# mLSTM cell and GELU MLP: the second chunk's weights all split, their sums moved beside the scores, the squares filled by ScalarE

## The chip, the cores and the metric

The kernel runs on one core of a Trainium2 chip. The metric is the device time in microseconds of the whole program: before the change, 455.98 us as the median of three runs (455.89 to 456.37). The trace is of one profiled execution, which took 455.72 us; all positions in this text are microseconds from the start of its span.

The engines are named as the profile names them: PE (matrix multiply; PEld is its weight load), DVE (VectorE), ACT (ScalarE), POOL (GpSimd) and SP (SyncE, which issues most transfers).

## The reference

Two blocks follow each other, all in float32.

```python
# q, k, v, o_gate: (B=4, H=8, S=768, D=40); i_gate, f_gate: (4, 8, 768)
for t in range(S):                                   # mLSTM cell, state C, n, m for each (b, h)
    m_new = max(f_gate[t] + m, i_gate[t])
    f, i = exp(f_gate[t] + m - m_new), exp(i_gate[t] - m_new);  m = m_new
    C = f * C + i * outer(v[t], k[t]);  n = f * n + i * k[t]
    y[t] = sigmoid(o_gate[t]) * (C @ q[t]) / max(abs(n @ q[t]), 1)
x = y.transpose(0, 2, 1, 3).reshape(3072, 320)       # heads side by side: H * D = 320
h = x @ w_in                                         # (320, 2048)
out = (h * sigmoid(1.702 * h)) @ w_out               # (2048, 320)
```

## The kernel before

The sequence is cut into six chunks of 128 steps (`w` = 0 to 5). The recurrence is turned into products within a chunk and a state carried between chunks, so a chunk of all four batches gives 512 rows of x, and the MLP of chunk `w` is run while the cell of chunk `w + 1` is computed beside it.

Each chunk has two stages on PE. `up` computes h transposed, in eight units `j`, each of two blocks of 128 columns of w_in, 512 rows wide. `down` multiplies the hidden values by w_out, in blocks; between the blocks the hand-written table `attention(w + 1)` puts the next chunk's cell: the carry, the scores, the values, the seams that turn the cell's output into the operand `xT`, and `split_x` and `split_on`, which prepare it for the next `up`. In chunk 0 both stages use plain float32 passes (`up`, 16 blocks of `down`); from chunk 1 on they are `up_fast` and `down_fast`, the latter with seven products of half matrices in place of eight, for which `w_out` is replaced by sums of its quarters (`t1`, `t2`, `t4` and a changed `w01`, made by `weight_sums(n)` on GpSimd) and the hidden values by sums (`hidden_difference`, `hidden_sums`, `last_sums`).

`up_fast` splits both operands. A float32 matrix is written as a high part, a low part and a difference, each in a form that PE multiplies in one pass of 512 columns. The 320 rows of w_in are two full blocks of 128 (`k` = 0, 1) and a rest of 64; the columns come in four pieces `n` of 512, two units to a piece. For each column block there are four main passes (high times high and low times low, for both k) and four side passes (two for the rest, two for difference times difference), so a unit has 16 passes. Main and side have PSUM banks of their own. Even units take theirs from the pool `ps_a`, odd ones from `ps_m`, two and four tiles in all, so unit j takes the banks that unit j - 2 had. ACT copies the scaled side product to the tile `g`, DVE adds the main product to it in one `scalar_tensor_tensor`, and ACT applies the GELU in place (`gelu_fast`). In chunk 1 pieces 2 and 3 are not split yet (`LATE`); their units j = 4 to 7 have `whole_passes`, float32 passes of 256 columns on w_in and xT, and only the rest's side passes.

The splits of w_in: `split_high(n)` on ACT, `split_diff(n)` on DVE, `split_low(n, engine)`. Highs stay in SBUF, and so do lows, but for piece 2. There is no room for the differences and low 2 in all stages: `keep` writes them to DRAM rows (`w_row`, 512 KB each, issued from ACT's queue), `fetch_diff` and `fetch_low` read them back through SP's queue in each `down` for the next chunk, into rooms that `rooms(w)` takes from the pools `gp` (eight tiles) and `sp` (four). The pools' other users are the `g` tiles, xT and the sums. `keep_last` copies low 3 to a place of its own.

The queries and keys of the next chunk are loaded in a layout with rows for four-step groups (`load_squares`: `q_sq`, `k_sq`), completed by `fill_squares` (two copies of 32 partitions each) and turned by `block_transposes` into `kT` and `qT`, on DVE, between the units j = 2 to 6.

Everything is in the order in which the text issues it (`tc.manual_schedule`): each engine runs its own queue in order, and the program adds semaphore waits. Transfers from SP's and ACT's queues take eight completion semaphores in turn; a transfer's issue waits until the transfer that last had its semaphore has landed. `wait_for(x)` makes GpSimd wait until x is written, by a tiny copy into the tile `mark`.

Order in chunk 1 before: `split_diff(1)`, `split_low(1, V)`, then the units; after j = 0 `gates(2)` on DVE and a wait of GpSimd for its end; after j = 0 to 3 one `weight_sums(j)` each; after j = 1 the row writes of differences 0 and 1; the transposes after j = 2 to 6. In its `down`, `split_high(2)`. In chunk 2 the other splits of pieces 2 and 3 come before j = 0 and after j = 1, with their row writes, and `keep_last` after j = 2.

Of the kernel before, what the change touches and what calls it, by code (L numbers as in the profile page):

```python
# [8 lines left out]
FP = mybir.dt.float32  # L9
FR = mybir.dt.float32r  # L10
# [21 lines left out]
def kernel(  # L32
# [81 lines left out]
    def fill_squares(t):  # L114

        x = t[:, 32:].rearrange("r (m d) -> r m d", d=D)
        for i in (0, 64):
            V.tensor_copy(out=x[i + 32:i + 64, :, 0:D - 32], in_=x[i:i + 32, :, 32:D])
# [281 lines left out]
    def block_transposes(w, n):  # L400
        b, (to, name, src) = n // 2, ((kT, "kT", k_sq), (qT, "qT", q_sq))[n % 2]
        if b == 0:
            fill_squares(src)
# [272 lines left out]
    LATE = (2, 3)  # L676

    def rooms(w):

        if w == 1:  # L680
            for n in (0, 1):
                w_diff[w, n] = sp.tile([128, 2, 512], FR, tag="g", name="w_diff")
        for c in range(2):
            xT[w, c] = (sp if w == 1 else gp).tile([128, 3, 2, L], FP, tag="g", name="xT")
        if w == 1:
            return
        for n in LATE[0:2 if w == 2 else 1]:
            w_low[w, n] = gp.tile([128, 2, 512], FR, tag="g", name="w_low")
        for n in (0, 2, 1, 3):
            w_diff[w, n] = sp.tile([128, 2, 512], FR, tag="g", name="w_diff")  # L690
# [5 lines left out]
    def split_diff(n):  # L696
        V.scalar_tensor_tensor(out=w_diff[2 if n in LATE else 1, n], in0=w_high[n], scalar=-1.0 - 1.0 / BASE,
                               in1=w_in[n], op0=OP.mult, op1=OP.add)

    def split_low(n, engine):  # L700
        if n not in LATE:
            w_low[n] = win.tile([128, 2, 512], FR, tag="wa" if n else "wb", name="w_low")
        engine.tensor_tensor(out=w_low[2, n] if n in LATE else w_low[n], in0=w_in[n], in1=w_high[n], op=OP.subtract)
# [5 lines left out]
    def keep_late(n):  # L709
        keep(w_diff_row, n, w_diff[2, n])  # L710
        if n == 2:
            keep(w_low_row, n, w_low[2, n])

    def keep_last():
        w_low[3] = work.tile([128, 2, 512], FR, tag="wx", bufs=1, name="w_low")
        A.copy(out=w_low[3], in_=w_low[2, 3])
# [46 lines left out]
    def gelu_fast(w, j, i):  # L763
        g = gs[w, j][:, i, :]
        A.activation(out=g, in_=g, func=AF.Gelu_apprx_sigmoid)  # L765
# [4 lines left out]
    def up_fast(w, j):  # L770
# [4 lines left out]
        whole = w == 1 and n in LATE  # L775
# [9 lines left out]
        def passes(which, i):  # L785
            for m in which:
                dst, k, a, x = parts[m]
                T.matmul(dst[i], a(i), x, start=(k == 0), stop=(k == (1 if whole else 3)))  # L788

        def whole_passes(i):  # L790
            for k in range(2):
                for c in range(2):
                    T.matmul(main[i][:, c * W // 2:(c + 1) * W // 2], w_in[n][:, k, col(i)],  # L793
                             xT[w, c][:, k].rearrange("p b t -> p (b t)"), start=(k == 0 and c == 0),
# [314 lines left out]
```

## Time and profile before

| | |
|---|---|
| median of three runs | 455.98 us |
| the profiled execution | 455.72 us, span 454.0 us |
| busy | PE 446.6 us (98%), DVE 342.6 (75%), ACT 214.0 (47%), POOL 132.5 (29%) |
| `up` of chunk 1 | 109.17 to 142.71 |
| `up` of chunks 2, 3, 4, 5 | 32.16, 29.54, 29.38, 29.40 us long |
| one g sum on DVE (L816) | 684 ns |
| one side copy on ACT (L812), one GELU (L765) | 591 ns, 629 ns |
| a difference or low of a piece on DVE (L697, L703) | 1.21 to 1.22 us |

A stage of `up` runs from PE's first pass for that chunk to its last; the `down` stage follows at once. The windows of the trace give each engine's busy time in such a stage; a PE busy time short of the window is idle PE. An engine other than PE may be idle without cost. In the chain of waits each piece is what the next one waited for, followed back from the end. Durations of neighbours on one engine overlap a little, so pairs are given start to start where it matters: two g sums take 1.20 us, two transposes 1.90.

### The profile page before, as it was taken

The page shows a single profiled execution, that of the slowest core. Times are in us where ns is not written, and L with a number is a line of the kernel's source. Part 1 is how long each engine was busy: PE and PEld are TensorE (multiplying, and loading weights), DVE is VectorE, ACT ScalarE, POOL GpSimd, SP SyncE. Part 2 cuts the span into 40 slices and gives each one's busy share as a digit, 9 for nine tenths or more (in the row PEclk, how much of TensorE's full clock was granted, in tenths as well). Part 3 has the DMA queues.
Part 4 walks back from the last instruction along what each step waited for, and adds up shares of the span by engine and source line. Part 5 has one row for each costly group of instructions (what it writes and reads, how often), then busy time and mean ns, then how long its engine had stood idle before and what let it go on. Part 6 is the DMA issues. An engine that isn't in the chain of part 4 may idle for free.

```text
span 454.0 us, 12115 instructions
## 1 busy us (share of the span) xinstructions
PE 446.6 (98%) x4967; PEld 388.8 (86%) x4967; DVE 342.6 (75%) x681; ACT 214.0 (47%) x471; POOL 132.5 (29%) x126
## 2 busy tenths in 40 slices
PE   8999999999999999998999999999999999999997
PEld 6877887776889999877999888999888999888996
DVE  6788999989799786879786789686789666733522
ACT  5686779601746701465900465900465910366100
POOL 5101317000496602334620044610035520035000
PEclk9999999999999999999999999999999999999999
DMA  8999999038669027858606987405998505700000
GB/s 169 200 304 192 229 222 195 1 73 205 93 144 166 4 61 206 226 95 155 81 19 142 309 132 158 64 17 139 304 127 148 86 17 142 228 37 1 1 30 29
DMA packets 129224, 58.49 MB, mean 129 GB/s; under 512 B 102048, under 2 KB 122480, under 8 KB 129168
## 3 DMA queue, kind: packets, MB, share of 16 engines
q1 hardware_dynamic: 120080, 53.28, 53.9%
q10 hardware_dynamic: 8768, 4.28, 4.1%
q8 instruction: 39, 0.64, 0.7%
q0 software_dynamic: 320, 0.15, 0.2%
q14 instruction: 17, 0.14, 0.1%
HBM read 47.53 MB, written 10.16 MB: 127 GB/s over the span
## 4 chain that ended last, share of the span: by engine, by line
PE 89%; DMA 4%; DVE 4%; SPq 1%; issue 1%; ACT 0%; ACTq 0%; DVEq 0%
PE p_out L879 34%; PE p_h L788 26%; PE p_h L638 6%; PE p_out L825 4%; PE p_h L793 3%; PE p_c L614 3%; PE p_s L471 2%; PE p_o L515 2%; PE p_i L523 2%; PE p_h L647 2%; DMA w_row<-w_diff 2%; PE p_t L396 1%; PE p_s L460 1%; DMA k_sq<-in_k_dram 1%; DMA wt<-m_row 1%
## 5 line engine op out<-in xcount | busy, mean ns | idle before, releaser
L816 DVE SCALAR_TENSOR_TENSOR g<-p_h,g 128x512 f32<-128x512 f32 x80 | 52.4, 684 | 32.0 <-ACT g L812 17.1
L879 PE MATMUL p_out<-w_out_sb,g 128*128 128x160 f32 x480 | 69.0, 300 | 1.1 <-ACT g L812 1.1
L765 ACT ACTIVATE g<-g 128x512 f32<-128x512 f32 x80 | 50.2, 629 | 38.8 <-DVE g L816 38.7
L879 PEld LDWEIGHTS p_out<-w_out_sb,g 128*128 128x128 f32 x480 | 66.3, 190 | 2.0 <-ACT g L812 1.6
L847 POOL TENSOR_TENSOR g<-g 128x512 f32<-128x512 f32 x20 | 25.9, 1302 | 125.4 <-ACT g L765 125.4
L812 ACT ACTIVATE g<-p_h 128x512 f32<-128x512 f32 x80 | 46.8, 591 | 30.6 <-PE p_h L788 28.5
L747 ACT ACTIVATE x_high<-xT 128x512 fp32r<-128x512 f32 x10 | 6.3, 631 | 112.6 <-DVE xT L584 112.6
L884 DVE TENSOR_TENSOR o_sb<-o_sb,p_out 128x160 f32<-128x160 f32 x70 | 21.1, 317 | 42.3 <-PE p_out L879 42.2
L788 PE MATMUL p_h<-x_rest,w_rest 128*128 128x512 f32 x160 | 50.4, 400 | 0.8 <-ACT g L812 0.7
L879 PE MATMUL p_out<-t_sb,s 128*128 128x160 f32 x320 | 47.1, 300 | 0.0
L879 PEld LDWEIGHTS p_out<-t_sb,s 128*128 128x128 f32 x320 | 44.4, 190 | 0.2
L788 PE MATMUL p_h<-x_low,w_low 128*128 128x512 f32 x144 | 43.9, 390 | 0.6 <-DVE x_low L757 0.6
L788 PE MATMUL p_h<-x_high,w_high 128*128 128x512 f32 x144 | 44.3, 394 | 0.0
L788 PE MATMUL p_h<-x_diff,w_diff 128*128 128x512 f32 x144 | 44.3, 394 | 0.0
L447 ACT ACTIVATE wt<-wt,cols 128x64 f32<-128x64 f32 x160 | 38.8, 333 | 0.1
L788 PEld LDWEIGHTS p_h<-x_rest,w_rest 128*128 128x128 f32 x160 | 29.7, 188 | 8.6 <-ACT g L812 1.1
L825 PE MATMUL p_out<-w_out_sb,g 128*128 128x320 f32 x128 | 35.7, 436 | 0.0
L788 PEld LDWEIGHTS p_h<-x_low,w_low 128*128 128x128 f32 x144 | 26.9, 188 | 6.7 <-DVE x_low L757 1.0
L788 PEld LDWEIGHTS p_h<-x_diff,w_diff 128*128 128x128 f32 x144 | 27.1, 188 | 6.3
L825 PEld LDWEIGHTS p_out<-w_out_sb,g 128*128 128x128 f32 x128 | 23.9, 190 | 9.6
L788 PEld LDWEIGHTS p_h<-x_high,w_high 128*128 128x128 f32 x144 | 26.8, 188 | 6.0 <-ACT x_high L747 0.4
L638 PE MATMUL p_h<-xT,w_in 128*128 128x256 f32 x128 | 29.6, 384 | 0.0
(194 smaller groups left out, 801.3 us busy)
## 6 DMA issues: line engine op xcount, KB each, us to landing
w_diff<-w_row SPq DMA_DIRECT2D x14, 512.0 KB, 4.5
wt<-m_row SPq DMA_DIRECT2D x20, 256.0 KB, 5.6
bits<-in_moe_w_in_dram SPq DMA_DIRECT2D x8, 512.0 KB, 8.7
out_dram<-o_sb SPq DMA_DIRECT2D x24, 160.0 KB, 2.4
q_sq<-in_q_dram SPq DMA_DIRECT2D x10, 320.0 KB, 7.8
eo<-in_o_gate_dram SPq DMA_DIRECT2D x5, 640.0 KB, 7.1
bits<-in_moe_w_out_dram SPq DMA_DIRECT2D x8, 320.0 KB, 5.9
q_sq<-x_row SPq DMA_DIRECT2D x10, 256.0 KB, 3.2
```

What stands on the lines that cost most here:

```text
L447: A.activation(out=x[:, h, :], in_=x[:, h, :], func=AF.Exp, scale=-1.0, bias=cols[w][:, c * PH + h:c * PH + h + 1])
L614: T.matmul(pc[i * 64:i * 64 + 64, x, j * D1:(j + 1) * D1], k_cols(w, t, c * PH + 2 * j + i), vw[w, c][t, 2 * j + i, :], start=True, stop=True)
L638: T.matmul(ph[j][i][:, t], w_in[f // 4][:, c, f % 4 * 128:f % 4 * 128 + 128], x[:, c, t], start=(first and c == 0 and n == 0), stop=(not f ...
L765: A.activation(out=g, in_=g, func=AF.Gelu_apprx_sigmoid)
L788: T.matmul(dst[i], a(i), x, start=(k == 0), stop=(k == (1 if whole else 3)))
L793: T.matmul(main[i][:, c * W // 2:(c + 1) * W // 2], w_in[n][:, k, col(i)], xT[w, c][:, k].rearrange("p b t -> p (b t)"), start=(k == 0 and ...
L812: A.activation(out=g[:, i, :], in_=side[i], func=AF.Copy, scale=-BASE)
L816: V.scalar_tensor_tensor(out=g[:, i, :], in0=main[i], scalar=1.0 if whole else 1.0 + 1.0 / BASE, in1=g[:, i, :], op0=OP.mult, op1=OP.add)
L825: T.matmul(po, gs[w, f // 2][:, f % 2, b * L:(b + 1) * L], w_out_sb[:, f, :], start=(f == 0), stop=(f == NF - 1))
L847: G.tensor_tensor(out=a10, in0=a00, in1=a10, op=OP.subtract)
L879: T.matmul(po, a(f), b[:, f, :], start=(f == 0), stop=(f == NH - 1))
L884: V.tensor_tensor(out=dst, in0=x, in1=po, op=OP.add)
```

## The change

Chunk 1 has no whole passes any more: pieces 2 and 3 are split in it, after j = 0 and j = 2 (highs) and after j = 1 and j = 2 (differences and lows, both on DVE), into four further `gp` tiles (`more_rooms`), which the g tiles of j = 4 to 7 take over afterwards. All five row writes are issued in chunk 1, after j = 1 (d0, d1), j = 2 (d2, l2) and j = 3 (d3), and `keep_last` after j = 3. Chunk 2 fetches everything back, as later chunks do.

`weight_sums` 0 and 1 go to chunk 0's `down` after block 8, sum 3 to after its block 12, each behind a `wait_for`; sum 2 follows j = 3 of chunk 1, behind a wait for low 3. `fill_squares` is done by ACT, for the keys after j = 1 and for the queries after j = 3 (in chunk 0, before block 0 of `down`). The output copies of chunk 0's `down` are done by ACT. In `up_fast` both side copies of a unit are issued before the GELUs of the unit before, where one GELU stood between them. Unit 0 takes its passes in the order 0, 1, 4, 6, 2, 7, 3, 5 (main 0 to 3 are high, high, low, low; side 4 to 7 are rest, rest, difference, difference) in place of 0, 1, 4, 2, 3, 5, 6, 7.

```diff
@@
 
         x = t[:, 32:].rearrange("r (m d) -> r m d", d=D)
         for i in (0, 64):
-            V.tensor_copy(out=x[i + 32:i + 64, :, 0:D - 32], in_=x[i:i + 32, :, 32:D])
+            A.copy(out=x[i + 32:i + 64, :, 0:D - 32], in_=x[i:i + 32, :, 32:D])
 
     def load(w, what, bs=slice(0, B)):
         hs = slice(bs.start * H, bs.stop * H)
@@
 
     def block_transposes(w, n):
         b, (to, name, src) = n // 2, ((kT, "kT", k_sq), (qT, "qT", q_sq))[n % 2]
-        if b == 0:
-            fill_squares(src)
         at, n = 32 + b * NP * 4 * D, NP * 4 * D
         to[w, b] = work.tile([128, NP, L], FP, tag=name, bufs=4, name=name)
         V.transpose(out=to[w, b].rearrange("d j (r c) -> d j c r", c=4),
@@
-    LATE = (2, 3)
 
     def rooms(w):
 
-        if w == 1:
-            for n in (0, 1):
-                w_diff[w, n] = sp.tile([128, 2, 512], FR, tag="g", name="w_diff")
+        w_diff.update({(w, n): sp.tile([128, 2, 512], FR, tag="g", name="w_diff") for n in ((0, 1) if w == 1 else ())})
         for c in range(2):
             xT[w, c] = (sp if w == 1 else gp).tile([128, 3, 2, L], FP, tag="g", name="xT")
-        if w == 1:
-            return
-        for n in LATE[0:2 if w == 2 else 1]:
-            w_low[w, n] = gp.tile([128, 2, 512], FR, tag="g", name="w_low")
-        for n in (0, 2, 1, 3):
-            w_diff[w, n] = sp.tile([128, 2, 512], FR, tag="g", name="w_diff")
+        if w > 1:
+            w_low[w, 2] = gp.tile([128, 2, 512], FR, tag="g", name="w_low")
+            w_diff.update({(w, n): sp.tile([128, 2, 512], FR, tag="g", name="w_diff") for n in (0, 2, 1, 3)})
+
+    def more_rooms(w):
+
+        w_low[w, 3], w_diff[w, 2], w_low[w, 2], w_diff[w, 3] = (gp.tile([128, 2, 512], FR, tag="g", name=name)
+                                                                for name in ("w_low", "w_diff", "w_low", "w_diff"))
 
     def split_high(n):
         w_high[n] = win.tile([128, 2, 512], FR, tag="wb" if n < 2 else "wa", name="w_high")
         A.activation(out=w_high[n], in_=w_in[n], func=AF.Copy, scale=BIAS)
 
     def split_diff(n):
-        V.scalar_tensor_tensor(out=w_diff[2 if n in LATE else 1, n], in0=w_high[n], scalar=-1.0 - 1.0 / BASE,
-                               in1=w_in[n], op0=OP.mult, op1=OP.add)
+        V.scalar_tensor_tensor(out=w_diff[1, n], in0=w_high[n], scalar=-1.0 - 1.0 / BASE, in1=w_in[n], op0=OP.mult,
+                               op1=OP.add)
 
     def split_low(n, engine):
-        if n not in LATE:
+        if n < 2:
             w_low[n] = win.tile([128, 2, 512], FR, tag="wa" if n else "wb", name="w_low")
-        engine.tensor_tensor(out=w_low[2, n] if n in LATE else w_low[n], in0=w_in[n], in1=w_high[n], op=OP.subtract)
+        engine.tensor_tensor(out=w_low[n] if n < 2 else w_low[1, n], in0=w_in[n], in1=w_high[n], op=OP.subtract)
 
     def keep(row, n, x):
         row[n] = rows.tile([128, 1024], FP, tag=f"{'d' if row is w_diff_row else 'l'}{n}", bufs=1, name="w_row")
         nc.scalar.dma_start(out=row[n], in_=x.rearrange("p c m -> p (c m)").bitcast(FP))
 
-    def keep_late(n):
-        keep(w_diff_row, n, w_diff[2, n])
-        if n == 2:
-            keep(w_low_row, n, w_low[2, n])
-
     def keep_last():
         w_low[3] = work.tile([128, 2, 512], FR, tag="wx", bufs=1, name="w_low")
-        A.copy(out=w_low[3], in_=w_low[2, 3])
+        A.copy(out=w_low[3], in_=w_low.pop((1, 3)))
 
     def split_rest():
 
@@
             V.scalar_tensor_tensor(out=x_rest[w][1][:, t], in0=x[:, 2], scalar=-1.0 / BASE, in1=x_rest[w][0][:, t],
                                    op0=OP.mult, op1=OP.subtract)
 
-    def gelu_fast(w, j, i):
-        g = gs[w, j][:, i, :]
-        A.activation(out=g, in_=g, func=AF.Gelu_apprx_sigmoid)
+    def gelu_fast(w, j):
+        for i in range(2):
+            g = gs[w, j][:, i, :]
+            A.activation(out=g, in_=g, func=AF.Gelu_apprx_sigmoid)
 
     def bank(name="p_h"):
         return ps_m.tile([128, W], FP, tag="m", name=name)
@@
         n = j // 2
         col = lambda i: slice((2 * j + i) % 4 * 128, (2 * j + i) % 4 * 128 + 128)
         low = w_low.get((w, n), w_low.get(n))
-        whole = w == 1 and n in LATE
         if j % 2:
             side, main = ([bank() for _ in range(2)] for _ in range(2))
         else:
@@
         parts += [(side, k, lambda i: w_rest[0][:, 2 * j + i], x) for k, x in enumerate(x_rest[w])]
         parts += [(side, 2 + k, lambda i, k=k: w_diff[w, n][:, k, col(i)], x_diff[w][k]) for k in range(2)]
 
-        def passes(which, i):
+        def passes(which, i, first=False, last=False):
             for m in which:
                 dst, k, a, x = parts[m]
-                T.matmul(dst[i], a(i), x, start=(k == 0), stop=(k == (1 if whole else 3)))
-
-        def whole_passes(i):
-            for k in range(2):
-                for c in range(2):
-                    T.matmul(main[i][:, c * W // 2:(c + 1) * W // 2], w_in[n][:, k, col(i)],
-                             xT[w, c][:, k].rearrange("p b t -> p (b t)"), start=(k == 0 and c == 0),
-                             stop=(k == 1 and c == 1))
-
-        if whole:
-            for i in range(2):
-                passes(range(4, 6), i)
-            for i in range(2):
-                whole_passes(i)
-        elif j:
+                T.matmul(dst[i], a(i), x, start=(first and m == which[0]), stop=(last and m == which[-1]))
+
+        if j:
             for which in (range(4, 8), range(4)):
                 for i in range(2):
-                    passes(which, i)
+                    passes(which, i, True, True)
         else:
-            for m in (0, 1, 4, 2, 3, 5, 6, 7):
+            order = (0, 1, 4, 6, 2, 7, 3, 5)
+            for m in order:
                 for i in range(2):
-                    passes((m,), i)
+                    passes((m,), i, m in (0, 4), m in (3, 5))
         g = gs[w, j] = gp.tile([128, 2, W], FP, tag="g", name="g")
         for i in range(2):
             A.activation(out=g[:, i, :], in_=side[i], func=AF.Copy, scale=-BASE)
-            if j and i == 0:
-                gelu_fast(w, j - 1, 1)
         for i in range(2):
-            V.scalar_tensor_tensor(out=g[:, i, :], in0=main[i], scalar=1.0 if whole else 1.0 + 1.0 / BASE, in1=g[:, i, :], op0=OP.mult,
+            V.scalar_tensor_tensor(out=g[:, i, :], in0=main[i], scalar=1.0 + 1.0 / BASE, in1=g[:, i, :], op0=OP.mult,
                                    op1=OP.add)
-        gelu_fast(w, j, 0)
+        if j:
+            gelu_fast(w, j - 1)
 
     def down(w, b, n):
         if n == 0:
@@
                      stop=(f == NF - 1))
         if n == NF // 4 - 1:
             o = op.tile([128, DM], FP, tag="o", name="o_sb")
-            V.tensor_copy(out=o, in_=po)
+            A.copy(out=o, in_=po)
             nc.sync.dma_start(out=out[b * S + w * L:b * S + (w + 1) * L, :], in_=o)
 
 
@@
             if w == 1:
                 split_diff(1)
                 split_low(1, V)
-            if w == 2:
-                split_diff(2)
-                split_low(2, G)
-                split_high(3)
-                split_low(3, G)
+                more_rooms(1)
             for j in range(NF // 2):
                 up_fast(w, j)
                 if more and j == 0:
                     gates(w + 1)
-                    if w == 1:
-                        wait_for(ends[w + 1])
-                if w == 1 and j < 4:
-                    weight_sums(j)
-                if w == 1 and j == 1:
-                    for n in (0, 1):
-                        keep(w_diff_row, n, w_diff[1, n])
-                if w == 2 and j < 2:
-                    if j:
+                if w == 1:
+                    if j == 0:
+                        split_high(2)
+                    if j == 1:
+                        for n in (0, 1):
+                            keep(w_diff_row, n, w_diff[1, n])
+                        split_diff(2)
+                        split_low(2, V)
+                    if j == 2:
+                        split_high(3)
+                        keep(w_diff_row, 2, w_diff[1, 2])
+                        keep(w_low_row, 2, w_low[1, 2])
                         split_diff(3)
-                    keep_late(2 + j)
-                if w == 2 and j == 2:
-                    keep_last()
+                        split_low(3, V)
+                        sums_from = w_low[1, 3].bitcast(FP)[:, 0, :]
+                    if j == 3:
+                        keep(w_diff_row, 3, w_diff[1, 3])
+                        keep_last()
+                        wait_for(sums_from)
+                        weight_sums(2)
+                if more and j in (1, 3):
+                    fill_squares(q_sq if j == 3 else k_sq)
                 if more and j == 1:
                     load(w + 1, "v")
                 if more and j == 2:
@@
                     hidden_difference(w, j - lag)
                 if j >= 6:
                     hidden_sums(w, (j - 6,), G)
-            gelu_fast(w, NF // 2 - 1, 1)
+            gelu_fast(w, NF // 2 - 1)
             if more:
                 load(w + 1, "o")
             hidden_sums(w, (2, 3), V)
@@
             blocks = down_fast(w, 0) + down_fast(w, 1)
         for i, block in enumerate(blocks):
             if w == 0 and i in (0, 4, 5):
+                if i == 0:
+                    fill_squares(q_sq)
                 convert((17, 18, 19)[max(i - 3, 0)])
                 if i == 0:
                     for n in (1, 3, 5, 7):
@@
                 load_squares(w + 2, "q")
             block()
             run(side.get(i, []))
+            if w == 0 and i in (8, 12):
+                wait_for(xT[1, 0][:, 0, 0, :] if i == 12 else w_out_flat[:, 9 * 512:])
+                for n in ((0, 1) if i == 8 else (3,)):
+                    weight_sums(n)
             if w == 0 and i == 5:
                 split_high(0)
                 split_rest()
@@
                 split_diff(0)
                 split_low(0, V)
                 split_rest_low()
-            if w == 1 and i == 5:
-                split_high(2)
             if w and more:
                 if i == 11:
                     fetch_diff(w + 1, (0, 1))
-                    if w > 1:
-                        fetch_low(w + 1)
+                    fetch_low(w + 1)
                     if w + 2 < NW:
                         load_squares(w + 2, "k")
                 if i == 13:
-                    if w > 1:
-                        fetch_diff(w + 1, (2, 3))
+                    fetch_diff(w + 1, (2, 3))
                     if w + 2 < NW:
                         load_squares(w + 2, "q")
 
```

## The prediction

> **What bounds it now.** I read the page first: PE is busy 98% of the span and holds 89% of the chain that ended last, so time is won only where PE issues fewer passes or idles less. Then the busy time by stage, for the `up` stages of chunks 1 (in two parts, around the change from split to whole passes), 2 and 3; columns are length, then PE, PEld, DVE, ACT, POOL busy (instructions), clock, DMA share, GB/s.
>
> ```profile
> 109.17:111.84 2.67, 2.11 (x10) 1.43 (x9) 2.60 (x7) 0.26 (x1) 0.00 (x0) 1.00 1.15 249
> 111.84:125.02 13.18, 13.18 (x57) 10.54 (x57) 10.80 (x25) 8.68 (x15) 4.99 (x3) 1.00 0.68 110
> 125.02:142.71 17.69, 17.69 (x83) 15.32 (x82) 17.28 (x21) 8.67 (x17) 17.53 (x11) 1.00 0.82 158
> 181.71:213.87 32.16, 30.23 (x132) 23.81 (x130) 27.10 (x48) 18.07 (x32) 13.03 (x9) 1.00 0.74 159
> 253.51:283.05 29.54, 29.54 (x131) 23.95 (x130) 25.51 (x48) 17.27 (x31) 10.39 (x8) 1.00 0.91 189
> ```
>
> An all-split chunk without idle PE takes 29.4 to 29.5 us (chunks 3, 4 and 5: 29.54, 29.38, 29.40), 3.675 a unit. Chunk 1 takes 33.54 and chunk 2 takes 32.16. The clock is 1.00 in every row. The chain of waits in chunk 1 says what the second half is made of:
>
> ```profile
> 111.84 14.28 PE p_h L788 x60
> 126.11 3.45 PE p_h L793 x16
> 129.57 0.92 PE p_h L788 x4
> ```
>
> A whole unit is 3.45 + 0.92 = 4.37 us. The chain in chunk 2 shows what its 2.6 us hang on:
>
> ```profile
> 194.56 1.15 DVE w_diff L697
> 195.72 7.28 DMA w_row<-w_diff
> 203.02 0.63 SPq L130
> ...
> 206.35 3.88 DMA wt<-m_row
> 210.24 0.82 issue
> 211.07 1.08 DVE qT L406
> ```
>
> The late splits and a 512 KB row write stand in it, and SP waits behind the write. The same wait in chunk 1, from the waits of SP's queue (total, times, longest):
>
> ```profile
> SPq L130 <- DMA w_row<-w_diff: 6.4, 2, 5.9
> ```
>
> The v load needs no w_row: the program's DMAs take eight completion semaphores in turn, and each waits on the issuing engine until its semaphore's previous user has landed. That matters below. The row writes (L707), from the tile's view, which also covers the reads back:
>
> ```profile
> L707 ACTq DMA_DIRECT2D w_row<-w_diff x4: 327/342/746, 120.3 to 195.7; - x4
> L707 ACTq DMA_DIRECT2D w_row<-w_low x1: 444/444/444, 188.2 to 188.2; - x1
> DMA to landing us min/median/max: 3.5/4.9/7.3
> ```
>
> The five writes alone, one by one: 6.4, 6.8 (chunk 1), 4.2, 5.0, 7.3 (chunk 2).
>
> **The change, part by part**, against the profiled execution of 455.72 us (span 454.0 and 1.72 around it; the median of the runs, 455.98, is 0.26 more).
>
> *Passes of chunk 1.* Units j=4..7 go from 17.69 us to 4 x 3.675 = 14.70: -2.99.
>
> *Order of unit 0.* PE starts at 109.17 and waits 0.56 for x_low, with slow first passes: units 0 to 3 take 15.85 us to 125.02 against 14.70. The new order (high, high, rest, diff 0, low 0, diff 1, low 1, rest) follows production: diff 1 is done by 111.07 (due 111.47), low 1 by 111.8 (due 111.9), the second rest by 112.4 (due 112.4). -1.15; at worst 0. It now needs w_diff[0] 0.9 to 1.4 us after the start. In chunk 3 that fetch is issued at 248.56 and lands 4.3 later, 252.9, needed about 254.7: nothing. Chunks 3 to 5 have no idle to win at the start.
>
> *Splits moved into chunk 1.* Two highs on ACT (1.05 each), two diffs and two lows on DVE (1.21 and 1.22): DVE +4.9. DVE loses the four square fills (3.46 + 1.87) and an output copy (0.48), so its 30.7 us from 109.17 become about 29.8, under PE's 29.4 plus the 1.3 by which its last g already trails. Fills and copies go to ACT, which is busy 18 to 20 us here: nothing, while it does not wait.
>
> *Row writes.* All five now leave from ACT's queue in chunk 1, and here a wait is added. By the instruction order, with durations from the trace: ACT copies side 0 until 114.0 and side 1 by 116.6, loads its table (1.28), runs two gelus to 118.9, then issues d0 at 118.9 and d1 at 119.4. d2 comes at 124.05, but shares its semaphore with d1: it leaves at 119.4 + 6.8 = 126.2, holding ACT 2.1 us. Behind it stand l2, side 3, gelu 2, d3, the copy of low 3 and the q fill, done about 131.5. Then side 4: its g tile is the room that d2 is written from, so it waits for d2's landing, 126.2 + 6.8 = 133.05, and is done at 134.15. Unit 6 takes unit 4's banks and is due at 109.17 + 6 x 3.675 = 131.2. PE idles 134.15 - 131.25 = +2.9. From both sides: the idle is the two landings' sum less 10.8. With 4.2 and 5.0 it is 0; with 7.3 twice it is 3.9. I take 6.8 twice, chunk 1's own row. Behind the stall, side 5 waits for l2 (127.0 + 6.8 = 133.8), side 7 for d3 (about 136.5): neither is later than PE. DVE ends 2.5 us after PE, against 1.2 in chunk 3, where the first total's sums are ready at 285.7 and used at 287.2; the 1.3 more use up that slack of 1.5 and cost nothing.
>
> The Trainium skill's page "DMA: Bandwidth & Descriptors", section "Anatomy of one DMA — SWDGE (gpsimd) path", fits one DMA as 2.0 us plus bytes at 436 GB/s, an estimate of 3.2 us for 512 KB; by it the sum would lose the 2.9 us of stall and end at 449.3. The five writes here took 4.2 to 7.3, so the rows decide. The same page says that the completion can take surprisingly long when the target is HBM, which these writes fit.
>
> *Chunk 2* loses both w_diff splits, the GpSimd lows, three row writes and the last copy, and fetches w_low and two w_diff more, as chunk 3 does. With chunk 3's instructions it should have its time: 32.16 to 29.54, -2.62; the bounds are 0 (the 1.9 us of PE idle stay, with another cause) and -2.78 (chunk 4's 29.38). The fetches wait behind nothing new; before, their median landing was 4.5.
>
> *Weight sums.* Four GpSimd operations of 3.0 us. Two run beside chunk 0's scores at about 86 to 92, one (t4) at about 106 to 109, w01 at about 126 to 129. What GpSimd does to DVE depends on the operation: the square fill beside such a sum took 3.0 us instead of 0.4:
>
> ```profile
> L118 DVE COPY k_sq<-k_sq x8: 417/418/3014, 126.0 to 338.3; 32x512 f32<-32x512 f32 x8
> ```
>
> while the kT transposes and the g sums from PSUM kept their 1.1 and 0.7. The fills leave DVE, so this row's cost goes. t4's neighbour is x_diff, with two SBUF inputs, on the way to unit 0's third step: between 0 (t4 done before) and 3.0 (blocked for all of it). t4 starts about 3 us before x_diff does, so I take 0.1. The Trainium skill, "SBUF — State Buffer", section "SBUF: two separate sides", calls the port pair that DVE and GpSimd share "an exclusive lock, not a bandwidth split", held for a whole instruction, also against a DVE operation with two SBUF inputs; by that rule alone t4 could cost x_diff its full 3.0, and the sum would be 455.1.
>
> *Gelu after both copies.* The side copies no longer wait for a gelu, which takes away the last wait of chunk 2 (1.14 at 213.87, ACT's g). It is inside the -2.62; elsewhere PE does not wait there: nothing.
>
> Sum: -2.99 - 1.15 + 2.9 - 2.62 + 0.1 = -3.76: 455.72 - 3.76 = 451.96, on the median 452.2.
>
> **Rivals.** *The rows land early* (chance 0.20). If d2 is written in time, as with chunk 2's 4.2 and 5.0, chunk 1 gives its full 4.14 and the total is -6.66: 449.3. For it: fewer transfers run at 119 to 126, as SP waits on d0. Against: chunk 1's own rows are 6.4 and 6.8.
>
> *The loss of chunk 2 isn't the splits'* (0.11). GpSimd's hidden sums stay there and DVE's gates stretched beside GpSimd work (one step took 1.29 instead of 0.24). If this and not the splits carries the idle, the -2.62 falls to about -0.5: 454.3. Against: chunk 3 has the same hidden sums and no idle.
>
> *Slower* (0.10): the row writes queue on each other. d1 to d3 are issued into traffic of v, raw and wt loads (DMA share 0.82 at 125 to 142), and ACT is stopped by every one. The gain without the stall is 6.66, so it is eaten when the two landings sum to 17.5, and measurably slower at 18.4, 9.2 us each; at 10 each the stall is 9.2 and the time 458.5. Nothing written to w_row took over 7.3, but three writes stand close together here, where there were two.
>
> **How the numbers follow.** The forecast has 0.55 (451 to 453.5: the stall from 1.7 to 3.9, t4 up to 0.4). 0.04 is left for a sum of small things that ends at no change. The range reaches from the early landing (449.3, less 0.3 for chunk 4's 29.38 and no t4: 449.0) to the case of chunk 2's idle staying, 454.4: it leaves out the slower case, the same case and some edges. About 0.2%, 0.9 us, is what a measurement of this kernel can tell from no change. Faster by more: 0.55 + 0.20 + 0.11 = 0.86, less 0.02 for the edge of the third case: 0.84. Within: 0.06. Slower: 0.10.
>
> **What would show it.** No L793 left; `up` of chunk 1 from 109.2 to about 141.6, with one PE idle of 2 to 3 us near 131, released by ACT's g, and ACT in turn by a w_row write; no wait for x_low at 111.8; `up` of chunk 2 at 29.5; SP's v loads waiting for w_row in chunk 1 only. Without the idle near 131 the first rival is right. With chunk 2 over 31 us the second is. The prediction is wrong if PE waits in chunks 3 to 5 (for w_diff, or for ACT's moved fills), or if chunk 1 starts later than 109.2 because of the sums beside the scores.

## The result

The changed kernel took 450.59 us (median of 4, 450.18 to 451.32) beside 456.17 for the one before: a ratio of 0.9876 (0.9856 to 0.9896), 5.6 us less. The profiled execution took 450.18, span 448.5. In two later sessions, on two chips, the same kernel had 453.95 (12 runs, 450.84 to 459.86; 0.994, 0.9906 to 0.9974) and 452.22 (6 runs, 451.17 to 453.22; 0.9903, 0.987 to 0.9935), while the kernel before stayed at 456.2 to 456.5. The ratios leave out runs more than 1.5% above a kernel's fastest; for the second session that hides a part of what the change does, so its spread is explained below too. Faster is right, and all three medians lie in the range; beside the forecast of 452.2 the first is 1.6 us lower, the second 1.75 higher and the third equal. The stall that I had forecast is not there.

PE's waits in the whole profile after are only these (engine, line, waited for, total, times, longest), none of them in an `up` stage:

```profile
PE p_idle L207 <- DVE one L213: 1.1, 1, 1.1
PE p_x L540 <- DVE y L488: 0.5, 1, 0.5
PE p_s L469 <- issue: 0.4, 1, 0.4
PE p_t L396 <- ACT qT L398: 0.2, 1, 0.2
```

The `up` stages of chunks 1, 2 and 3, in the columns of the stage table shown before; all three are full:

```profile
109.90:139.45 29.55, 29.55 (x130) 24.07 (x129) 28.19 (x49) 23.16 (x41) 12.24 (x10) 1.00 0.76 192
178.60:208.11 29.51, 29.51 (x130) 24.14 (x130) 23.22 (x43) 20.27 (x35) 10.38 (x8) 1.00 0.93 192
247.26:276.75 29.49, 29.49 (x132) 24.15 (x131) 24.23 (x44) 20.28 (x35) 10.39 (x8) 1.00 1.00 206
```

Counted from the first pass of a stage to the first of the next, chunk 1's `up` went from 33.37 to 29.55 (-3.82) and chunk 2's from 32.16 to 29.51 (-2.65). Against them stand 0.73 by which chunk 1's `up` starts later (0.82 is there already at the start of chunk 0's `down`, 66.82 against 66.00 in the chain), and +0.75 in chunk 3's `down`, where the chain has PE idle with nothing that it waits for (292.00, 0.44, "issue"). Small differences in the other stages bring the span to -5.5.

Where the forecast stall went is seen in the timeline of ACT in chunk 1 (start, duration, engine, line, operation, in brackets the idle time before and its releaser):

```profile
116.37 0.58 ACT L793 ACTIVATE g<-p_h 128x512 f32<-128x512 f32 x1
116.61 0.34 ACTq L704 DMA_DIRECT2D w_row<-w_diff  x1
116.85 0.59 ACT L793 ACTIVATE g<-p_h 128x512 f32<-128x512 f32 x1
117.00 0.45 ACTq L704 DMA_DIRECT2D w_row<-w_diff  x1
117.46 1.28 ACT L758 ACT_TABLE_LOAD   x1
118.75 1.16 ACT L758 ACTIVATE g<-g 128x512 f32<-128x512 f32 x2
...
123.46 1.06 ACT L691 ACTIVATE w_high<-w_in 128x1024 fp32r<-128x1024 f32 x1
123.49 0.33 ACTq L704 DMA_DIRECT2D w_row<-w_diff  x1
123.86 0.45 ACTq L704 DMA_DIRECT2D w_row<-w_low  x1
...
130.48 1.09 ACT L793 ACTIVATE g<-p_h 128x512 f32<-128x512 f32 x2 [1.14 <-PE p_h L780]
```

The row writes d0 and d1 stand behind the first GELUs in ACT's order, but they leave at 116.61 and 117.00, 1.7 us and more before those GELUs run: ACT's queue passes the GELUs on and issues the transfers without waiting for them to finish. d0 landed after 2.7 us, against 6.1 for the same row before (the 6.4 of the prediction is the median of the pair's 6.1 and 6.8); d1 landed after 4.2, at 121.18, so d2, which has its semaphore, left at 123.49 without a wait. d2 landed after 6.4, at 129.9, and the side copy of unit 4 at 130.48 was released by PE.

### The profile page after: what moved, and what is told of

Its sections match the earlier page's. It is cut to its first block, busy times and chain, and to the rows that moved or that the text cites. A ratio compares the mean times of both kernels' runs of the same rounds, so it can differ in the third digit from the quotient of the medians.

```text
span 448.5 us, 12127 instructions
## 1 busy us (share of the span) xinstructions
PE 443.2 (99%) x4951; PEld 386.8 (86%) x4951; DVE 326.9 (73%) x661; ACT 228.8 (51%) x493; POOL 126.1 (28%) x126
## 4 chain that ended last, share of the span: by engine, by line
PE 98%; DVE 1%; issue 0%; ACT 0%; DVEq 0%
PE p_out L859 35%; PE p_h L780 33%; PE p_out L805 8%; PE p_h L636 6%; PE p_c L612 3%; PE p_o L513 2%; PE p_s L469 2%; PE p_i L521 2%; PE p_h L645 2%; PE p_t L396 1%; PE p_s L458 1%; PE p_w L425 1%; PE p_idle L207 0%; PE p_o L503 0%; PE p_w L437 0%
## 5 line engine op out<-in xcount | busy, mean ns | idle before, releaser
L793 ACT ACTIVATE g<-p_h 128x512 f32<-128x512 f32 x80 | 44.8, 597 | 46.7 <-PE p_h L780 46.6
L780 PE MATMUL p_h<-x_diff,w_diff 128*128 128x512 f32 x160 | 50.1, 394 | 0.0
L780 PE MATMUL p_h<-x_low,w_low 128*128 128x512 f32 x160 | 49.3, 389 | 0.0
L780 PE MATMUL p_h<-x_high,w_high 128*128 128x512 f32 x160 | 49.3, 394 | 0.0
L780 PE MATMUL p_h<-x_rest,w_rest 128*128 128x512 f32 x160 | 49.2, 394 | 0.0
L758 ACT ACTIVATE g<-g 128x512 f32<-128x512 f32 x80 | 46.4, 626 | 2.9 <-DVE g L795 2.6
L780 PEld LDWEIGHTS p_h<-x_diff,w_diff 128*128 128x128 f32 x160 | 30.1, 188 | 6.9
L780 PEld LDWEIGHTS p_h<-x_low,w_low 128*128 128x128 f32 x160 | 30.0, 188 | 6.4
L780 PEld LDWEIGHTS p_h<-x_high,w_high 128*128 128x128 f32 x160 | 29.8, 188 | 6.5 <-ACT x_high L739 0.3
```

The source lines that it names most:

```text
L780: T.matmul(dst[i], a(i), x, start=(first and m == which[0]), stop=(last and m == which[-1]))
L793: A.activation(out=g[:, i, :], in_=side[i], func=AF.Copy, scale=-BASE)
```

## The experiments

My theory after the result: the three gains on PE (passes, order of unit 0, chunk 2) are as predicted, the stall is missing because the writes leave earlier, and the mechanism of the stall (a shared semaphore or a room that waits for a landing) exists. The rivals: that no such wait exists; that chunk 2's gain is not the splits'; and, from the second session on, that the changed kernel's spread is the chip's clock and not the kernel's.

**The changed kernel again (after_again, after_third).** No edit.

> The changed kernel once more, beside which the others are read. Both theories: ratio to before 0.986 to 0.989, up of chunk 1 29.4 to 29.6 us with PE never idle. It also tells whether the start is a matter of the execution: in the first profile of the changed kernel the down stage of chunk 0 began at 66.82, before at 66.00, though nothing in the text changed ahead of it. Theory one (the first loads' landing varies by itself): somewhere between 65.5 and 67, and not twice the same. Theory two (the change moves something at the start): 66.8 again.

Both ratios, 0.994 and 0.9903, miss the forecast 0.986 to 0.989. The first of these runs gave the 453.95 with the spread of 9 us. The span of its profile is 458.2 us, with `up` of chunk 1 at 29.5 us and one large new wait, in chunk 0's `down`. The waits of 50 to 100 us:

```profile
POOL vw L598 <- ACT cols L377: 18.0, 1, 18.0
ACT q_sq L118 <- DMA q_sq<-in_q_dram: 5.4, 2, 4.1
PE p_c L612 <- POOL vw L598: 4.9, 1, 4.9
```

Read from below: PE waits 4.9 us to start the carry, for GpSimd's values; GpSimd for the columns, from ACT; and ACT for the load of q_sq, in the fill of the queries' square, which the change put ahead of chunk 0's first block of `down`, on ACT. The load of the second half of q_sq left SP's queue late, at 66.13 against 59.27 in the first profile; it took 9.2 us here and 10.0 there. The timeline of ACT there, first of the changed kernel's first profile, then of this one:

```profile
69.33 0.61 ACT L118 COPY q_sq<-q_sq 32x512 f32<-32x512 f32 x1 [0.82 <-DMA q_sq<-in_q_dram]
...
72.55 0.26 ACT L377 ACTIVATE cols<-cols 128x64 f32<-128x64 f32 x1
```

```profile
75.41 0.61 ACT L118 COPY q_sq<-q_sq 32x512 f32<-32x512 f32 x1 [1.31 <-DMA q_sq<-in_q_dram]
...
78.57 0.26 ACT L377 ACTIVATE cols<-cols 128x64 f32<-128x64 f32 x1
```

And what follows is dearer than the wait, as the stage table of this profile shows (the column behind the busy times is the granted clock):

```profile
74.00:80.00 6.00, 1.46 (x6) 0.71 (x4) 3.06 (x5) 4.60 (x11) 1.09 (x1) 1.00 1.15 237
80.00:86.00 6.00, 5.62 (x132) 4.94 (x133) 5.83 (x9) 6.00 (x27) 5.40 (x6) 0.50 0.06 13
86.00:90.00 4.00, 4.00 (x14) 2.69 (x14) 3.04 (x5) 4.00 (x10) 2.36 (x2) 0.90 0.00 0
```

After the idle time the granted clock is 0.50 for 6 us: the carry takes 3.65 us instead of 2.00 and the next blocks 8.05 instead of 6.66. So 4.9 us of waiting cost 8.2 (chunk 0's `down` 51.42 us against 43.25). The start of the second fill against PE's wait for vw, over all profiles with this fill on ACT (their `down` began at 66.0 to 66.7):

| kernel | second fill starts | PE's wait | clock after | `down` of chunk 0 |
|---|---|---|---|---|
| after | 69.33 | none | 1.00 | 43.25 |
| rows_together | 70.28 | 0.2 | 1.00 | 43.79 |
| after_third | 70.85 | 1.0 | 1.00 | 45.00 |
| only_fill0_on_act | 71.12 | 1.3 | 1.00 | 45.32 |
| rows_late | 72.34 | 2.3 | 0.50 | 47.11 |
| first_order | 73.97 | 3.7 | 0.50 | 48.94 |
| after_again | 75.41 | 4.9 | 0.50 | 51.42 |

Up to about 70 the load is hidden; from there nearly each microsecond is PE's, and in the three profiles with 2.3 us of waiting or more the clock falls as well.

**That fill back on DVE (fill0_on_dve, fill0_on_dve_again, after_third).**

```diff
             if w == 0 and i in (0, 4, 5):
-                if i == 0:
-                    fill_squares(q_sq)
                 convert((17, 18, 19)[max(i - 3, 0)])
                 if i == 0:
+                    fill_squares(q_sq, V.tensor_copy)
...
```

(`fill_squares` takes the copy as an argument here, ACT's where none is given.)

> The changed kernel, but chunk 0's fill of the queries' square is done by DVE, behind the conversion of piece 17, as before the change; ACT keeps the other fills. Theory one (the spread of the changed kernel comes from ACT, which waits in this fill for the load of q_sq and holds the columns, GpSimd's vw and PE's carry behind it): no wait of PE for vw at the start of chunk 0's down, no fall of the granted clock there, all runs within about 1 us and their median at 449.5 to 450.5, ratio 0.985 to 0.988. Theory two (the spread has another cause, such as the clock giving way under denser passes): the runs still spread from 451 to 459.

> The changed kernel a third time, beside fill0_on_dve_again on the same chip. Theory one (ACT's wait for the load of q_sq in chunk 0 decides): its runs lie over those of fill0_on_dve_again wherever q_sq lands later than about 70.5 us (the two copies, two conversions and the table load take 5.0 us to the columns, vw another 1.4, and PE needs vw at about 75.5); with landing at 69 to 70 both are the same. Theory two (the chip alone): both spread alike.

> As before under this name: the changed kernel with chunk 0's fill of the queries' square on DVE. Theory one: all runs at 450 to 452 wherever the chip puts the loads, no wait of PE for vw. Theory two: spread as in the changed kernel.

450.92 (4 runs, 450.35 to 451.82), ratio 0.9886 (0.987 to 0.9902); in the other session 451.35 (6 runs, 450.52 to 453.34), 0.9891 (0.9857 to 0.9924), beside 452.22 of the changed kernel on the same chip. No profile shows PE waiting for vw; ACT's columns come at 70.06 and 70.60. Where q_sq lands early the two kernels are alike, and on the chip of the later session their intervals overlap, so that this version is better is not shown by the times there. For the cause the profiles speak: in the kernels with this fill on DVE the second half of q_sq landed as late as 71.4 (fill0_on_dve_gelu_between) and 72.8 (fill0_on_dve_late_kept), ACT's columns still came by 70.6, and PE did not wait for vw, while with the fill on ACT a landing at 72.3 (rows_late) cost 2.3 us of waiting. The version was not run on the chip with the largest spread.

**The fill alone on ACT, in the kernel before (only_fill0_on_act).**

```diff
             if w == 0 and i in (0, 4, 5):
+                if i == 0:
+                    fill_squares(q_sq, A.copy)
                 convert((17, 18, 19)[max(i - 3, 0)])
...
```

> The kernel before, with one edit alone: chunk 0's fill of the queries' square goes to ACT ahead of the conversion of piece 17. Theory one (this fill on ACT is what makes the changed kernel's time spread): the same spread appears here, runs from 456 to 465, median 1 to 4 us over the kernel before, with PE waiting for vw and the clock at 0.5 behind that. Theory two: 456 to 457 as the kernel before.

456.53 (6 runs, 455.88 to 457.7) beside 456.15, ratio 1.0012 (0.9997 to 1.0027): a miss in size. The profile has the wait of theory one, with 1.3 us, but q_sq landed at 71.1 there and not at 75, and the times do not stand clear of the kernel before. The edit makes a kernel depend on a landing; how late that is, is the chip's and the execution's.

**Row writes later, and all together (rows_late, rows_together).** The keeps of difference 2 and low 2 are put behind `keep_last`; or those of differences 0 and 1 beside them after unit 2.

```diff
 # rows_late                                    # rows_together
-  keep(w_diff_row, 2, ...)   (after j = 2)      -  for n in (0, 1): keep(w_diff_row, n, ...)   (after j = 1)
-  keep(w_low_row, 2, ...)                       +  for n in (0, 1): keep(w_diff_row, n, ...)   (after j = 2)
   keep_last()
+  keep(w_diff_row, 2, ...); keep(w_low_row, 2, ...)
```

> The row writes of difference 2 and low 2 are issued after the copy of low 3, some 3.5 us later (about 127.0 instead of 123.5). Theory one (unit 4's g tile waits for the landing of difference 2's row, as predicted, and the forecast stall is only missing because the writes left earlier than I had them): landing at 127.0 + 6.4 = 133.4, side copy of unit 4 done at 134.5, PE idle 2.0 to 2.8 us before unit 6, total 2 to 3 us over the changed kernel (about 453). Theory two (the room is not held by the landing, or a write alone lands in 3 us): no idle, time of the changed kernel within 0.3 us.

> Differences 0 and 1 are written after unit 2 together with difference 2 and low 2, four writes of 512 KB in a row at about 123.5 to 124.8. Theory one (the writes share the bandwidth and land after each other): difference 2 lands 8 to 10 us after its issue, at 132.5 to 134.5, PE idles 1.5 to 3.5 us before unit 6, total 1.5 to 3.5 over the changed kernel. Theory two (a write's landing does not depend on the others near it, 6.4 us): landing at 130.8, no idle.

Both ran on the chip of the large spread, so their totals (459.16 and 456.69, beside 453.95) hold the other wait as well; the stage is read instead. In both PE idles before unit 6, 3.3 and 3.0 us, released by the side copy of unit 4, in `up` of chunk 1. ACT's timeline in rows_together shows the cause:

```profile
131.55 0.33 ACTq L704 DMA_DIRECT2D w_row<-w_diff  x1
131.97 1.05 ACT L708 CAST w_low<-w_low 128x1024 fp32r<-128x1024 f32 x1 [3.47 <-DMA w_row<-w_diff]
133.04 1.25 ACT L118 COPY q_sq<-q_sq 32x512 f32<-32x512 f32 x2
134.32 1.08 ACT L793 ACTIVATE g<-p_h 128x512 f32<-128x512 f32 x2
```

Four writes in a row land after 6.5 to 8.4 us. ACT's queue issues d3 only at 131.55, since d3 there has the semaphore of d1, which landed at 131.47, and the copy of low 3, the fill and the side copy stand behind it; PE goes on at 135.46. It is the kind of wait that I predicted, at its price (2.9), on another pair of writes. Theory one's landing for d2 came true as well (8.2 us after its issue, at 132.73), but the path to PE went over d3. In rows_late it is low 2's write: it has the semaphore of a load of v on SP's queue, which landed at 136.22, and left at 136.24; the fill and the side copy behind it started at 136.66 and 137.94. So the idle there is not that of theory one, which had d2's landing as its cause.

The wait for the room itself, the other half of the prediction's stall, is in the profile of after_again, without any edit: there d2 landed after 7.0 us, at 138.66, and ACT's timeline has the side copy of unit 4 waiting for it:

```profile
138.74 1.09 ACT L793 ACTIVATE g<-p_h 128x512 f32<-128x512 f32 x2 [1.19 <-DMA w_row<-w_diff]
```

It came early enough for PE, which has no wait in that stage.

**Pieces 2 and 3 kept late (fill0_on_dve_late_kept).** The kernel before with the other parts of the change (sums, fills but for chunk 0's, output copies, GELU order, unit 0's order).

```diff
-                if w == 1 and j < 4: weight_sums(j)
+                if w == 1 and j == 3: weight_sums(2)
-            for m in (0, 1, 4, 2, 3, 5, 6, 7):
+            for m in (0, 1, 4, 6, 2, 7, 3, 5):
...
```

> As fill0_on_dve, but pieces 2 and 3 stay late: whole passes for units 4 to 7 of chunk 1, the splits and row writes of the second half in chunk 2 as before; sums, fills, copies, GELU order and the order of unit 0 are those of the change. Theory one (the sum of the prediction holds term by term): up of chunk 1 at 32.4 us (29.4 + 2.99), up of chunk 2 still over 31 us, since its splits and rows are back; total 4.5 to 5.5 over fill0_on_dve, about 455. Theory two (chunk 2's loss came from the GELU between the copies and from GpSimd, not from the splits): chunk 2 at 29.4 to 30 here too, total 3 over fill0_on_dve, about 453.

454.43 (5 runs, 453.93 to 454.93), ratio 0.9961 (0.9948 to 0.9973), 3.5 over fill0_on_dve: between the two theories. `up` of chunk 1 takes 32.67 us against 29.75, +2.92, as the 2.99 said. Chunk 2 takes 31.32 against 29.48, +1.84, with two waits in it (the waits of PE from 105 to 215):

```profile
PE p_out L877 <- ACT g L811: 0.7, 1, 0.7
PE p_h L787 <- ACT g L811: 0.6, 1, 0.6
```

So of chunk 2's 2.65 some 1.8 us hang on the splits and row writes, and the rest, 0.84, on the other parts. The two make 4.8 where the profiles differ by 3.9 (spans 452.5 and 448.6): fill0_on_dve loses 0.6 in chunk 3's `down`, as the other kernels without whole passes do (0.6 to 2.2), and this one, like the kernel before, does not (39.15); the rest lies ahead of chunk 1.

**Weight sums back in chunk 1 (fill0_on_dve_sums_in_up).**

```diff
-            if w == 0 and i in (8, 12): ... weight_sums(n)
+                    if j == 0: wait_for(ends[w + 1])
+                    if j < 4: weight_sums(j)
...
```

> As fill0_on_dve, but all four weight sums run in chunk 1's up again, behind the gates, about 120 to 132. Theory one (a GpSimd operation on two SBUF tiles stops DVE's operations with two SBUF inputs): differences and lows 2 and 3, 1.2 us each alone, take up to 3 to 4 us beside a sum, the g sums behind them come late, PE idles 2 to 5 us in chunk 1. Theory two (DVE's operations beside the sums keep their durations, as its transposes and PSUM sums did before): within 0.5 us of fill0_on_dve.

459.04 (6 runs, 457.85 to 459.8), ratio 1.006 (1.0045 to 1.0074): 8.1 over fill0_on_dve, and slower than the kernel before. Theory one, and dearer than I put it. DVE's timeline has the splits of pieces 2 and 3 beside the four sums (GpSimd, 120.35 to 134.96), and PE's waits give the price:

```profile
121.00 3.41 DVE L694 SCALAR_TENSOR_TENSOR w_diff<-w_high,w_in 128x1024 fp32r<-128x1024 f32 x1
124.34 3.96 DVE L700 TENSOR_TENSOR w_low<-w_in,w_high 128x1024 fp32r<-128x1024 f32 x1
...
129.48 2.71 DVE L694 SCALAR_TENSOR_TENSOR w_diff<-w_high,w_in 128x1024 fp32r<-128x1024 f32 x1
132.11 3.94 DVE L700 TENSOR_TENSOR w_low<-w_in,w_high 128x1024 fp32r<-128x1024 f32 x1
```

```profile
PE p_h L780 <- DVE g L795: 6.0, 2, 3.2
PE p_h L780 <- ACT g L793: 0.8, 1, 0.8
```

Four operations of 1.2 us take 14 in all, and three of the sums 3.8 to 3.9 instead of 2.9; the g sums from PSUM between them keep their 1.27 a pair. The Trainium skill, "SBUF — State Buffer", section "SBUF: two separate sides", says it so: a DVE operation with two SBUF inputs and a GpSimd operation that reads SBUF exclude each other for a whole instruction; these four durations agree with it. So the move of the sums, which the prediction gave a cost of 0.1 and no gain, is what makes the splits in chunk 1 pay: with the sums beside them the kernel is slower than before.

**Old order of unit 0 (first_order, fill0_on_dve_first_order).**

```diff
-            order = (0, 1, 4, 6, 2, 7, 3, 5)
+            order = (0, 1, 4, 2, 3, 5, 6, 7)
...
```

> Unit 0 takes its passes in the old order (0, 1, 4, 2, 3, 5, 6, 7); all else is the changed kernel. Theory one (the old order's wait for x_low was worth 1.15 us in chunk 1): PE waits for x_low near 111.8 again, total 0.6 to 1.2 us over the changed kernel, chunks 2 to 5 unchanged. Theory two (in the changed kernel x_low would be in time also for the old order): no difference over 0.3 us.

> As fill0_on_dve, with unit 0's passes in the old order. Theory one: up of chunk 1 is longer by 0.6 to 1.2 us (PE waits for x_low), chunks 2 to 5 the same, total 0.6 to 1.2 over fill0_on_dve_again. Theory two (x_low is early enough now): within 0.3.

On the chip of the spread the first has the wait for q_sq above all (458.17); the second gave 453.98 (12 runs, 453.0 to 455.32), 0.9944 (0.9925 to 0.9963), 2.6 over fill0_on_dve_again. Chunk 1's `up` is 30.60 against 29.59, +1.0 as predicted, and 30.47 in the other session. But here chunks 3, 4 and 5 lose too (30.01, 29.85, 30.48 against 29.5), which neither theory had, while in first_order's profile they did not (29.48 to 29.53). In chunk 3 the second x_low starts 1.35 us after the stage's first pass here and 0.76 us after it there. PE's wait for it is listed in this profile for chunks 1 and 5:

```profile
PE p_h L780 <- DVE x_low L749: 1.1, 2, 0.6
```

**One GELU between the side copies again (fill0_on_dve_gelu_between).**

```diff
             A.activation(out=g[:, i, :], in_=side[i], func=AF.Copy, scale=-BASE)
+            if j and i == 0:
+                gelu_fast(w, j - 1, 1)
...
-        if j:
-            gelu_fast(w, j - 1)
+        gelu_fast(w, j, 0)
```

> As fill0_on_dve, with one GELU of the unit before put between the two side copies again. Theory one (the side copies wait for DVE only where DVE is late, so in chunk 1, whose DVE is full): the last side copy of chunk 1 comes 1 to 2 us later and PE waits for it at the first block of down, 0.5 to 1.5 us over fill0_on_dve_again; chunks 2 to 5 under 0.2 each. Theory two (the order of GELU and copies does not matter once chunk 2's splits are gone): within 0.3.

453.55 (11 runs, 452.88 to 454.76), 0.9937 (0.9917 to 0.9958), 2.2 over fill0_on_dve_again. `up` of chunk 1 takes 32.32 us, +2.7, chunks 2 to 5 the same 29.5. That is theory one's place, at twice its price and in the middle of the stage, not at its end:

```profile
PE p_h L779 <- ACT g L792: 2.0, 2, 1.6
```

But the chain of waits there names a cause that neither theory had:

```profile
120.11 0.61 DVE g L796
...
120.74 0.35 ACT g L757
...
121.13 6.57 DMA w_row<-w_diff
...
127.72 0.33 ACTq L704
...
134.74 2.35 PE p_h L779 x9
```

The edit also puts a GELU of unit 1 itself ahead of the row writes, as in the kernel before, and that one waits for DVE's g sum. So d0 and d1 leave at 120.75 and 121.13, where fill0_on_dve_again has 117.43 and 117.81; d1 lands only at 127.70, d2 waits for its semaphore until 127.72, and ACT stands behind d2:

```profile
128.58 0.60 ACT L792 ACTIVATE g<-p_h 128x512 f32<-128x512 f32 x1 [2.47 <-DMA w_row<-w_diff]
```

This is the stall of the prediction on the very pair of writes that it named. What the order of GELUs and copies costs without it was not tried.

## Why the prediction was right, and where not

*Passes of chunk 1, -2.99.* Right: 2.92 with the late pieces back. It is only kept with the sums elsewhere (8.1 us) and with the GELUs behind both copies (2.7 in this stage): parts to which the prediction gave nothing ("elsewhere PE does not wait there: nothing"). They are covers, and what they cost when gone is about as large as the gain, or larger.

*Order of unit 0, -1.15.* Right in chunk 1 (1.0). "Chunks 3 to 5 have no idle to win at the start" was true of the trace before and is true in one profile of the changed kernel with the old order; in the other that order loses 0.4 to 1.0 in each. Why x_low comes later there is open.

*Row writes, +2.9.* The step that failed. Both waits in it exist: that of d2 for d1's semaphore in fill0_on_dve_gelu_between, where PE waits 2.0 us, and that of the side copy for d2's landing in after_again. What was wrong is when d1 is down. I had it leave at 119.4, behind the end of two GELUs, and land after 6.8, at 126.2; it left at 117.0 and landed after 4.2, at 121.2, before d2 was due; SP's loads of v had no wait for a row write either. Of these 5.0 us 2.4 are the issue's and 2.6 the landing's. For the issue the trace before had the answer: there the writes left when a GELU had just been started.

```profile
120.28 0.63 ACT L765 ACTIVATE g<-g 128x512 f32<-128x512 f32 x1 [1.56 <-DVE g L816]
120.29 1.13 ACTq L707 DMA_DIRECT2D w_row<-w_diff  x2
```

The landing goes with the time of issue. In the ten profiles in which d0 left 6.7 to 8.1 us after the first pass of chunk 1's `up` it landed in 2.6 to 2.7 us; in the four in which it left 10.9 to 13.6 us after that pass, before among them, it took 5.9 to 6.5. What it meets there is not shown. The first rival came true, by little: d2 had landed 0.6 us before the copy that needed it, and 0.2 before it in after_third; in after_again the copy waited for it.

*Chunk 2, -2.62.* Right in size (2.65). Of the cause, 1.8 us are the splits' and rows' and 0.84 the other parts'.

*Fills to ACT: "nothing, while it does not wait".* The other step that failed, and it was mine to see: in chunk 0 ACT does wait, for a load, and the columns, vw and PE's carry stand behind. In the trace before, the same fill ran on DVE at 74.33, for two loads issued from 61.42 on that landed at 71.1 and 73.1; ACT's columns came at 69.56, ahead of both. The two lines:

```profile
69.56 0.26 ACT L377 ACTIVATE cols<-cols 128x64 f32<-128x64 f32 x1
74.33 2.13 DVE L118 COPY q_sq<-q_sq 32x512 f32<-32x512 f32 x2
```

The condition stood in the sentence, but I did not set the two times beside each other. It is the true slower case of this change: 8 us in the worst profile, on another engine and in another chunk than the one that I had named.

*Weight sums beside the scores, +0.1.* In the right place: t4 ran 106.75 to 109.67, and x_diff's pair beside it took 1.05 instead of 0.74; PE did not wait for it. Chunk 1 did start later than 109.2, at 109.90, but not because of the sums: the lag was there at the start of chunk 0's `down`, before them.

*The sum.* That the first time lies 1.6 us from the forecast and not 2.9 is luck in part: 0.73 and 0.75 us lost at the start and in chunk 3's `down`, which the prediction did not have, stand against the stall that did not come.

What stays open is first the loss of 0.6 to 2.2 us in chunk 3's `down`, in each kernel that has no whole passes left. A part of it, 0.2 to 1.2 us a profile, is idle time of PE for which the profile names nothing waited for. The transfers tell more. In the window 289.5 to 292.5 of the changed kernel's first profile, where PE idles from 292.00 to 292.44, there is a single one, of the kind that the profile calls instruction (number, MB, share):

```profile
q8 instruction: 1, 0.02, 2.1%
```

It is 16 KB long and lands 1.5 us before PE goes on. In all profiles of these kernels together there are 18 such idle times of over 0.1 us in chunk 3's `down`, and each ends 1.2 to 1.5 us after such a transfer has landed. So PE seems to wait there for its next instructions; that is argued from these times alone, and why it happens in this `down` and only without whole passes is not shown. The other open point is the 0.8 at the start: chunk 0's `down` begins (first pass) at 65.84 in the profile before, at 66.65, 66.68 and 66.09 in the three of the changed kernel, and at 66.0 to 66.9 in the experiments, among them 66.02 in only_fill0_on_act, whose program is the old one up to there; it varies by execution, and whether a part of it is the change's can't be told.

## What to carry to other kernels

When an operation is moved to another engine, ask first what it waits for and who stands behind it there: a fill of 0.6 us that waits for a load is harmless on an engine with slack and takes PE with it on another. Take a transfer's issue to be at the moment when its queue reaches it, not when the work ahead of it ends; a wait ahead of it does hold it, as the GELU does in fill0_on_dve_gelu_between. And cost the parts of a change together: the place of the sums and the order of the GELUs had no gain in my sum for chunk 1, and without the one the kernel is 8 us slower, without the other 2.

## What the runs showed of the hardware

The granted clock fell to 0.50 with idle of PE of 2.3 and 3.3 us (both in rows_late), 3.7 (first_order) and 4.9 (after_again), for 3.4 us in the first three cases and 6.8 in the last, where the kernel before had 1.00 in every window read. In first_order it fell only at 80.35, 1.4 us after PE had gone on. After 3.0 us in rows_together it stayed at 1.00:

```profile
132.00:136.00 4.00, 1.01 (x5) 0.53 (x4) 1.05 (x2) 3.90 (x7) 2.07 (x2) 1.00 1.02 309
136.00:142.00 6.00, 6.00 (x27) 4.88 (x26) 6.00 (x9) 5.29 (x12) 4.50 (x4) 1.00 0.58 131
```

The Trainium skill, "TensorE: Matmul & The Clock Gate", section "Part 1: The HAM clock gate (the "warmup" mystery)", gives an activity window of about 3.4 us that runs freely, and the half clock after at least one idle window. The half clock agrees, and so do its lengths, one and two such windows; but 2.3 and 3.3 us of idle were enough here, less than a window, so in this the measurement decides. Why 2.3 us was enough where 3.0 was not, no run here tested. In after_again a wait of 4.9 us cost 8.2 in all.
